# q, k, v loads on two DMA queues and matmuls on a zero tile between the first attention stages of a fused retention and MLP kernel

## The chip, the cores and the metric

One Trainium2 chip, one core of it. The metric is the time of one execution on the device in microseconds (us); lower is better. Most executions agree within 0.3%; each run is marked fast or slow, and only fast runs are compared. A profile is one more execution with the hardware profiler. Its "span" runs from the first to the last instruction and is about 2 us shorter than the time (252.3 against 254.3 here).

Names in the profile: PE is the matmul engine, PEld its weight loads, DVE, ACT and POOL the vector, scalar and general engines, SP the sync engine, which only issues DMA transfers. A DMA transfer issued by POOL goes to queue q0 ("software"), one issued by SP to q1 ("hardware"). L103 is line 103 of the kernel.

## The reference

```python
q, k, v: [4, 8, 768, 64] float32      # batch, heads, time, head size
gamma = 1 - 2 ** (-5 - arange(8))     # decay per head
for t in range(768):
    state = gamma * state + outer(k[t], v[t])
    y[t]  = q[t] @ state / sqrt(64)
x = y as [3072, 512]
h = x @ w_in                          # [512, 2048]
out = (h * cos(h)) @ w_out            # [2048, 512]
```

## The kernel before

The recurrence is computed in blocks of 128 time steps. A "pair" is one block of two batch items; there are 12 pairs. Each pair has six loads of 256 KB (q, k, v, two batch items each). Pairs 0 and 1 go through the attention first. Then six groups follow, of 16 steps each; a step computes one block of the first product (`unit_f`) and part of the second one for the group before (`unit_o`), and the attention of the next two pairs is woven in: `conv` (scaling of q and v on POOL), `stage_t` (transposes), `stage_a`/`stage_m` (masked scores), `stage_y`.

Every load is issued by POOL, and POOL does its work strictly in program order:

```python
    def load_pair(p):
        bp, c = divmod(p, NC)
        for t, src in ((qf, q), (kf, k), (vf, v)):
            for b in range(2):
                nc.gpsimd.dma_start(
                    out=t[p % PRE][:, b],
                    in_=src[2 * bp + b, :, ds(c * C, C)].rearrange("h t d -> t h d"))
# ... load_pair(0), constants (cut)
    load_pair(1)
    for r in range(2):
        load_w_in(r)
    conv_q(0, nc.vector)
    conv_k(0, True)
    conv_v(0, nc.gpsimd)
    stage_t(0)
    for r in range(2, 4):
        load_w_in(r)
    m0 = stage_a(0)
    conv_q(1, nc.vector)
    conv_k(1, True)
    conv_v(1, nc.gpsimd)
    for it in m0:
        stage_m(0, it)
    stage_t(1)
    stage_y(0)
    m1 = stage_a(1)
    for it in m1:
        stage_m(1, it)
    load_pair(2)
    load_pair(3)
    stage_y(1)
    for r in range(4):
        load_w_out(r)
    load_pair(4)

    def conv(p):
        conv_q(p, nc.gpsimd)
        conv_k(p, False)
        conv_v(p, nc.gpsimd)

    todo = []
    for g in range(NG + 1):
        for s in range(16):
            hf, r = divmod(s, 8)
            p = 2 * (g + 1) + hf
            if g < NG:
                unit_f(g, s)
            if g > 0:
                unit_o(g - 1, *divmod(s, 4))
            if p < NP:
                if r == 0:
                    conv(p)
                elif r == 1:
                    stage_t(p)
# ... stage_a, stage_m at r 2 and 3 (cut)
                elif r == 6:
                    stage_y(p)
                    if p + 3 < NP:
                        load_pair(p + 3)
```

A q, k or v load moves pieces of 64 float32, 256 bytes. A `w_in` or `w_out` load reads 1 MB and converts it to bfloat16, 512 KB written.

## Time and profile before

| | before |
|---|---|
| time, median | 254.37 us (254.3 to 255.47) |
| span of the profile | 252.3 us |
| PE idle before pair 2 | 22.2 us |
| POOL's multiply of q of pair 2 starts | 49.89 us |
| first transposes of pair 2 on PE | 51.00 us |
| first `unit_f` of the second group | 72.94 us |

Four rows of the page's slices of the kernel before: the span in 40 equal parts of 6.3 us, each digit the busy share in tenths, PEclk the granted clock of PE in tenths, GB/s what the DMA engines moved.

```profile
PE   0447400099798999999999999999999999999994
POOL 8999476498999999998330423000000000000000
PEclk9999755569999999999999999999999999999999
GB/s 110 218 212 207 233 218 209 206 235 219 221 158 222 158 194 223 188 168 221 108 0 44 42 44 1 42 47 42 3 42 44 42 0 44 42 42 42 44 83 83
```

PE is nearly full from the 13th slice on, and idle in slices 6 to 8; the DMA engines are full all through that gap, at 206 to 218 GB/s, and POOL is at work too. So the question is what holds up PE's start. The waits view of the kernel before (who waited for whom: us in total, how often, longest) has one long wait of PE:

```profile
PE bank_67 L162 <- POOL qs_98 L141: 22.2, 1, 22.2
```

qs_98 is q of pair 2, scaled on POOL. The timeline of POOL in the kernel before (start, length, what, and in brackets the idle time before it and what ended it) shows what POOL did instead:

```profile
30.92 0.88 POOL L103 DMA_DIRECT2D kf_89<-in_k_dram  x1 [0.32 <-DMA qf_83<-in_q_dram]
...
46.11 0.88 POOL L103 DMA_DIRECT2D vf_95<-in_v_dram  x1 [1.25 <-DMA w_out_sb<-in_moe_w_out_dram]
48.99 0.88 POOL L103 DMA_DIRECT2D vf_95<-in_v_dram  x1 [2.00 <-DMA w_out_sb<-in_moe_w_out_dram]
49.89 2.05 POOL L141 TENSOR_TENSOR qs_98<-qf_83,gq 128x512 bf16<-128x512 f32 x2
```

POOL issues loads and waits between them. The wait in front of kf_89 ended with the landing of qf_83, issued eight loads earlier; the same holds at every such wait, so at most eight of POOL's loads are under way. The last load ahead of the multiply, vf_95, is number 38 and could be issued when number 30, a w_out load, had landed. The data of pair 2 were there much earlier: the chain of waits has the landing of its last load (vf_93) at 36.7 us. The windows view of the kernel before (busy us of each engine in a stretch, granted clock, DMA share, GB/s) shows the engines' rate in that time:

```profile
core 0: us, PE busy (x) PEld busy (x) DVE busy (x) ACT busy (x) POOL busy (x), PEclk, DMA share, GB/s
30.00:40.00 10.00, 0.00 (x0) 0.00 (x0) 1.29 (x2) 0.00 (x0) 7.01 (x9) 0.56 1.05 219
40.00:50.00 10.00, 0.00 (x0) 0.00 (x0) 0.00 (x0) 0.00 (x0) 5.54 (x8) 0.50 1.19 205
```

And the DMA view for the first 49.9 us of the kernel before, that is up to the multiply:

```profile
DMA packets 5690, 10.06 MB, mean 202 GB/s; under 512 B 495, under 2 KB 4153, under 8 KB 5689
```

10.06 MB had been moved when PE could go on. The view counts bytes written, so a `w_in` or `w_out` load counts as 0.52 MB although it reads twice that; all MB and GB/s below are meant so.

### The profile page before, as it was taken

What the parts mean: (1) busy time and instruction counts of PE and PEld (TensorE: products, weight loads), DVE (VectorE), ACT (ScalarE), POOL (GpSimd) and SP (SyncE); (2) the same over time, 40 slices, a digit from 0 to 9 for tenths busy, and PEclk for the clock granted to TensorE, in tenths of its full rate; (3) what the DMA queues carried; (4) which work ended last, traced back from release to release, by engine and by line L of the source; (5) the groups of instructions that cost most, each with busy time, mean ns of one, the idle gap of its engine ahead of it and who ended that gap; (6) DMA issues with size and microseconds to landing.
All of it is one profiled execution on the core that took longest, in us unless ns stands there. A gap on an engine that the chain in (4) does not pass through costs nothing.

```text
span 252.3 us, 4113 instructions
## 1 busy us (share of the span) xinstructions
PE 204.9 (81%) x1640; PEld 107.4 (43%) x1664; DVE 119.1 (47%) x191; ACT 120.1 (48%) x174; POOL 116.8 (46%) x132
## 2 busy tenths in 40 slices
PE   0447400099798999999999999999999999999994
PEld 0336200055354455554455545545555454444441
DVE  4166320029685666347555665375556633343100
ACT  2434500047665556464565565645655554445210
POOL 8999476498999999998330423000000000000000
PEclk9999755569999999999999999999999999999999
DMA  4999999999979689779301110111011101111122
GB/s 110 218 212 207 233 218 209 206 235 219 221 158 222 158 194 223 188 168 221 108 0 44 42 44 1 42 47 42 3 42 44 42 0 44 42 42 42 44 83 83
DMA packets 13458, 29.62 MB, mean 117 GB/s; under 512 B 1664, under 2 KB 5760, under 8 KB 13440
## 3 DMA queue, kind: packets, MB, share of 16 engines
q0 software_dynamic: 9984, 23.07, 44.1%
q1 hardware_dynamic: 3456, 6.29, 6.7%
q8 instruction: 13, 0.21, 0.3%
q14 instruction: 5, 0.04, 0.1%
HBM read 27.26 MB, written 6.29 MB: 133 GB/s over the span
## 4 chain that ended last, share of the span: by engine, by line
PE 67%; POOL 15%; DMA 10%; issue 5%; DVE 1%; ACT 0%; POOLq 0%; ACTq 0%
PE bank_66 L246 14%; PE bank_63 L246 6%; PE bank_65 L232 5%; DMA vf_93<-in_v_dram 5%; PE bank_64 L232 5%; DMA w_out_sb<-in_moe_w_out_dram 5%; PE bank_69 L232 4%; PE bank_67 L232 4%; PE bank_68 L232 4%; PE bank_67 L246 4%; PE bank_63 L232 3%; PE bank_68 L246 3%; PE bank_69 L246 3%; POOL vs_103 L146 1%; POOL vs_102 L146 1%
## 5 line engine op out<-in xcount | busy, mean ns | idle before, releaser
L232 PEld LDWEIGHTS <-w_in_sb 128*128 128x128 bf16 x384 | 36.0, 99 | 40.8 <-issue 2.0
L246 PEld LDWEIGHTS <-gt_120 128*128 128x128 bf16 x192 | 18.8, 98 | 22.6
L246 PEld LDWEIGHTS <-gt_121 128*128 128x128 bf16 x192 | 18.8, 98 | 22.6
L246 PE MATMUL bank_66<-w_out_sb,gt_120 128*128 128x512 bf16 x96 | 24.6, 379 | 0.0
L162 PE MATMUL bank_67<-ident,qs_98 128*128 128x128 bf16 x8 | 1.0, 264 | 22.2 <-POOL qs_98 L141 22.2
L235 ACT ACTIVATE cosb_122<-bank_65,halfpi 128x512 bf16<-128x512 f32 x14 | 9.6, 687 | 14.5 <-PE bank_65 L232 14.5
L246 PE MATMUL bank_66<-w_out_sb,gt_121 128*128 128x512 bf16 x64 | 16.4, 379 | 0.0
L246 PE MATMUL bank_63<-w_out_sb,gt_120 128*128 128x512 bf16 x63 | 16.2, 379 | 0.1
L163 ACT COPY qkt_107<-bank_67 128x1024 bf16<-128x1024 bf16 x2 | 2.0, 1012 | 23.2 <-PE bank_67 L162 23.2
L162 PEld LDWEIGHTS <-qs_98 128*128 128x128 bf16 x32 | 2.4, 106 | 23.6 <-POOL qs_98 L141 22.9
L246 PE MATMUL bank_67<-w_out_sb,gt_121 128*128 128x512 bf16 x48 | 11.8, 379 | 0.0
L236 DVE TENSOR_TENSOR gt_120<-bank_69,cosb_124 128x512 bf16<-128x512 f32 x3 | 2.0, 683 | 19.9 <-ACT cosb_124 L235 19.9
L232 PE MATMUL bank_69<-xt_119,w_in_sb 128*128 128x512 bf16 x44 | 11.3, 379 | 0.0
L225 DVE CAST stb_117<-st_ps 64x512 bf16<-64x512 f32 x12 | 8.2, 687 | 5.7 <-PE st_ps L220 5.5
L235 ACT ACTIVATE cosb_124<-bank_64,halfpi 128x512 bf16<-128x512 f32 x9 | 6.2, 687 | 9.7 <-PE bank_64 L232 9.7
L232 PE MATMUL bank_63<-xt_118,w_in_sb 128*128 128x512 bf16 x40 | 10.3, 379 | 0.0
L232 PE MATMUL bank_65<-xt_119,w_in_sb 128*128 128x512 bf16 x34 | 8.8, 379 | 0.3 <-issue 0.3
L232 PE MATMUL bank_67<-xt_119,w_in_sb 128*128 128x512 bf16 x34 | 8.8, 379 | 0.3 <-issue 0.3
L232 PE MATMUL bank_64<-xt_119,w_in_sb 128*128 128x512 bf16 x34 | 8.8, 379 | 0.3 <-issue 0.3
L232 PE MATMUL bank_65<-xt_118,w_in_sb 128*128 128x512 bf16 x28 | 8.2, 405 | 0.9 <-issue 0.7
L246 PE MATMUL bank_68<-w_out_sb,gt_120 128*128 128x512 bf16 x32 | 8.2, 379 | 0.0
L246 PE MATMUL bank_69<-w_out_sb,gt_121 128*128 128x512 bf16 x32 | 8.2, 379 | 0.0
(324 smaller groups left out, 517.8 us busy)
## 6 DMA issues: line engine op xcount, KB each, us to landing
w_in_sb<-in_moe_w_in_dram POOLq DMA_DIRECT2D x4, 512.0 KB, 9.8
w_out_sb<-in_moe_w_out_dram POOLq DMA_DIRECT2D x4, 512.0 KB, 12.1
qf_81<-in_q_dram POOLq DMA_DIRECT2D x6, 256.0 KB, 4.3
kf_86<-in_k_dram POOLq DMA_DIRECT2D x6, 256.0 KB, 5.0
vf_91<-in_v_dram POOLq DMA_DIRECT2D x6, 256.0 KB, 5.5
qf_82<-in_q_dram POOLq DMA_DIRECT2D x6, 256.0 KB, 5.1
kf_87<-in_k_dram POOLq DMA_DIRECT2D x6, 256.0 KB, 5.8
vf_92<-in_v_dram POOLq DMA_DIRECT2D x6, 256.0 KB, 6.4
```

The costliest lines, as they stand in the source:

```text
L146: eng.tensor_tensor(out=vs[p % NB][:, b], in0=vf[p % PRE][:, b], in1=bc(gk, p % NC), op=ALU.mult)
L162: nc.tensor.transpose(tr[:, w, a, :], src[:, b, 2 * a : 2 * a + 2, :], ident)
L163: nc.scalar.copy(out=qkt[n][:, b], in_=tr)
L225: nc.vector.tensor_copy(out=stb[(p + 1) % 2][ts(j, 64), :, :, ts(j, 64)], in_=st_ps[ts(j, 64)])
L232: nc.tensor.matmul(bank, lhsT=w_in_sb[:, i, ts(f, 128)], rhs=xt[g % 2][:, i, :], start=(i == 0), stop=(i == KIN - 1))
L235: nc.scalar.activation(out=cb, in_=bank, func=AF.Sin, bias=halfpi)
L236: nc.vector.tensor_tensor(out=gt[g % 2][:, f, :], in0=bank, in1=cb, op=ALU.mult)
L246: nc.tensor.matmul(bank, lhsT=gt[g % 2][:, f, ts(j, 128)], rhs=w_out_sb[:, f, :], start=(f == 0), stop=(f == KOUT - 1))
```

## The change

The intent is twofold: to take half of the loads off POOL, so that issuing and waiting for them costs POOL less and two queues feed the DMA engines; and to keep PE's clock up through the short attention stages of pairs 0 and 1 with matmuls on a tile of zeros. With it come a new place for the w_in loads in the program and one copy moved from ACT to DVE. The diff:

```diff
--- before.py
+++ after.py
@@ -67,6 +67,15 @@
     st_ps = psum.tile([128, 2, HP, D], FP32, name="st_ps")
 
     ident = sb([128, 128], BF16, "ident")
+    zer = sb([128, 512], BF16, "zer")
+    nc.vector.memset(zer, 0.0)
+
+    def warm(n):
+        bank = banks.take()
+        for _ in range(n):
+            nc.tensor.matmul(bank, lhsT=zer[:, :128], rhs=zer, start=True, stop=True)
+        banks.give(bank)
+
     mask = sb([128, 128], BF16, "mask")
     pos = sb([128, NC], FP32, "pos")
     lgp = sb([128, NC, H], FP32, "lgp")
@@ -98,9 +107,11 @@
 
     def load_pair(p):
         bp, c = divmod(p, NC)
-        for t, src in ((qf, q), (kf, k), (vf, v)):
+        for t, src, engs in ((qf, q, (nc.sync, nc.sync)),
+                             (kf, k, (nc.gpsimd, nc.gpsimd)),
+                             (vf, v, (nc.sync, nc.gpsimd))):
             for b in range(2):
-                nc.gpsimd.dma_start(
+                engs[b].dma_start(
                     out=t[p % PRE][:, b],
                     in_=src[2 * bp + b, :, ds(c * C, C)].rearrange("h t d -> t h d"))
 
@@ -152,7 +163,7 @@
         else:
             nc.vector.tensor_copy(out=ks[p % NB], in_=kf[p % PRE])
 
-    def stage_t(p):
+    def stage_t(p, split):
         n = p % NB
         for b in range(2):
             bank = banks.take()
@@ -160,7 +171,10 @@
             for w, src in enumerate((qs[n], ks[n])):
                 for a in range(HP):
                     nc.tensor.transpose(tr[:, w, a, :], src[:, b, 2 * a : 2 * a + 2, :], ident)
-            nc.scalar.copy(out=qkt[n][:, b], in_=tr)
+            if split and b == 1:
+                nc.vector.tensor_copy(out=qkt[n][:, b], in_=tr)
+            else:
+                nc.scalar.copy(out=qkt[n][:, b], in_=tr)
             banks.give(bank)
 
     def qt(n, b, a):
@@ -254,28 +268,34 @@
 
 
     load_pair(1)
-    for r in range(2):
-        load_w_in(r)
+    load_w_in(0)
+    warm(14)
     conv_q(0, nc.vector)
     conv_k(0, True)
     conv_v(0, nc.gpsimd)
-    stage_t(0)
-    for r in range(2, 4):
-        load_w_in(r)
+    stage_t(0, True)
+    warm(3)
+    load_w_in(1)
+    load_w_in(2)
     m0 = stage_a(0)
+    warm(6)
+    for it in m0:
+        stage_m(0, it)
     conv_q(1, nc.vector)
     conv_k(1, True)
     conv_v(1, nc.gpsimd)
-    for it in m0:
-        stage_m(0, it)
-    stage_t(1)
+    load_w_in(3)
+    stage_t(1, True)
+    warm(3)
     stage_y(0)
     m1 = stage_a(1)
+    warm(8)
     for it in m1:
         stage_m(1, it)
     load_pair(2)
     load_pair(3)
     stage_y(1)
+    warm(4)
     for r in range(4):
         load_w_out(r)
     load_pair(4)
@@ -298,7 +318,7 @@
                 if r == 0:
                     conv(p)
                 elif r == 1:
-                    stage_t(p)
+                    stage_t(p, False)
                 elif r == 2:
                     todo = stage_a(p)
                     stage_m(p, todo[0])
```

## The prediction

> **What bounds the kernel.** From about 78 us to the end (252.3) the chain of waits is almost all PE: groups of four 128x512 matmuls at 0.86 us, no idle. Nothing in the change touches that part. What can move is when it starts. The timeline shows PE idle from 28.8 to 51.0 us; what ends the wait is qs_98 on POOL (the waits view: 22.2 us for this one wait). POOL could not start that multiply before 49.89 although q, k, v of pair 2 had all landed by about 37: in program order it stands behind the loads of pair 3, w_out and pair 4, and each POOL load waits for the one eight issues earlier (kf_89 waits for qf_83; the last vf_95 waits for the second w_out load). So POOL reaches the multiply when load 30 of 38 has landed. In that time the DMA engines are full: the windows view shows a DMA share of 1.05 to 1.21 and 205 to 221 GB/s from 12 to 60 us. A 256 KB q/k/v load costs 1.2 us of all 16 engines, a w load (512 KB written) 2.55 us. After that, 51 to 73 us, the first 16 output blocks take 21.9 us for about 18.1 us of PE work, because PE runs at half clock until 56.4 and because POOL needs 9.5 us per pair (4.1 multiply + 5.4 issue).
>
> **What the change does.** Per pair, three of six loads leave POOL for SP. Ahead of the multiply of pair 2 POOL now issues 23 loads, not 38, and with the same rule of eight waits for load 15 (a k of pair 3), with no w_out load ahead of it: 11 q/k/v loads (13 us) and 4 w_in (10.2 us) plus start, issue and landing. SP runs ahead with the q and half the v of pairs 0 to 6 (up to 21 loads) and competes. If a load costs the same on SP, and all 21 go first, the multiply starts near 54; if they share, near 40. The trace suggests sharing: POOL's 4 KB packets take 159 ns for some 50 to 80 packets after a pause and 302 to 314 ns in steady flow, so a single queue seems to leave half the engines' capacity unused. The Trainium skill ("DMA: Bandwidth & Descriptors", "Issuing engines are not separate DMA queues") says more issuing engines save only sequencer time; I expect total GB/s above 221 in this head nevertheless. POOL per pair falls to about 6.8 us, so it stops delaying PE afterwards.
>
> **Warm matmuls.** 38 of 128x512, at most 0.43 us each, stand in a head that ends around 25 to 30 us, before PE waits anyway. The last four end more than 8 us before pair 2 arrives, so PE is cold again by then ("TensorE: Matmul & The Clock Gate", "The HAM clock gate": half clock after an idle window of about 3.4 us; here 0.5 was granted after the stall began, till 56.4). I expect 0 us from them, within 1. The copy moved from ACT to DVE: also 0.
>
> **Sum.** Multiply of pair 2: 49.9 -> about 40.5 (9.4 us gained, range 0 to 16). First 16 blocks: 21.9 -> about 19.5 (2.4 gained). Rest unchanged at 179.4 + 2 outside the span. 254.3 - 11.8 = **242.5 us**, range 234 to 252. Chances: faster by over 2% 0.82, within 0.14, slower 0.04.
>
> **Signs.** Right: qs of pair 2 starts at 36 to 45 us, PE idle before it is under 17 us, head traffic over 240 GB/s, PE still shows 0.86 us groups at the end. Wrong: the SP loads' 256-byte pieces take the engines from POOL's queue (w_in late, k of pair 3 landing after 50), or SP is slow (over 3 us per load) and POOL waits for q of pair 2 or 4.

## The result, and the profile after

| | before | after |
|---|---|---|
| time, median | 254.37 us | 246.57 us (246.19 to 247.1) |
| span of the profile | 252.3 us | 244.9 us |
| PE idle before pair 2 | 22.2 us | 13.0 us |
| multiply of q of pair 2 starts | 49.89 us | 42.84 us |
| first transposes of pair 2 (A) | 51.00 us | 43.95 us |
| first `unit_f` of the second group (B) | 72.94 us | 65.77 us |
| from A to B | 21.94 us | 21.82 us |
| from B to the end of the span | 179.4 us | 179.1 us |

The ratio is 0.9685 (95% interval 0.9653 to 0.9717). A ratio is the mean time of one kernel's fast runs over that of the other's of the same rounds, so it is not quite the ratio of the medians. The changed kernel is 3.1% faster. The table says where: of 7.4 us of span, 7.05 are gained before PE starts pair 2, 0.1 between A and B, 0.2 after.

The same slices of the changed kernel (6.1 us each):

```profile
PE   7358900897999999999999999999999999999993
POOL 8620885985089994373306015000000000000000
PEclk9875985599999999999999999999999999999999
GB/s 157 220 203 197 193 227 208 195 211 225 216 200 246 231 170 158 185 108 195 43 102 88 29 161 57 1 44 45 43 3 43 43 45 11 32 43 45 73 56 86
```

PE now restarts in the eighth slice. The row of GB/s is not higher than before; POOL's row has a hole in slices 3 and 4. The waits view and POOL's timeline of the changed kernel:

```profile
PE bank_65 L173 <- POOL qs_100 L152: 13.0, 1, 13.0
```

```profile
12.45 1.56 POOL L119 DMA_DIRECT2D w_in_sb<-in_moe_w_in_dram  x2
25.38 2.04 POOL L157 TENSOR_TENSOR vs_105<-vf_94,gk 128x512 bf16<-128x512 f32 x2 [11.37 <-DMA vf_94<-in_v_dram]
27.37 0.81 POOL L119 DMA_DIRECT2D w_in_sb<-in_moe_w_in_dram  x1
...
41.95 0.88 POOL L114 DMA_DIRECT2D vf_97<-in_v_dram  x1 [0.32 <-DMA kf_91<-in_k_dram]
42.84 2.05 POOL L152 TENSOR_TENSOR qs_100<-qf_85,gq 128x512 bf16<-128x512 f32 x2
```

The multiply (now qs_100) stands behind 23 loads, and the last one, vf_97, waited for kf_91, a k of pair 3 and number 15 of POOL's loads; no w_out load had to land first. The new hole is the line at 25.38: POOL stood for 11.37 us until v of pair 1 came, whose first half is now loaded by SP. The windows and the DMA view of the changed kernel for the time up to its multiply:

```profile
30.00:40.00 10.00, 1.00 (x5) 0.27 (x3) 1.98 (x3) 1.37 (x2) 6.93 (x9) 0.73 1.13 220
40.00:50.00 10.00, 6.04 (x43) 3.53 (x44) 1.55 (x3) 3.12 (x4) 8.34 (x10) 0.58 1.19 196
50.00:60.00 10.00, 8.60 (x106) 4.83 (x104) 7.81 (x13) 7.58 (x12) 8.66 (x9) 1.00 1.15 220
```

```profile
DMA packets 15554, 8.59 MB, mean 201 GB/s; under 512 B 12499, under 2 KB 14785, under 8 KB 15553
q0 software_dynamic: 3310, 5.49, 67.1%
q1 hardware_dynamic: 12243, 3.09, 43.3%
```

The mean rate up to the multiply is 201 GB/s, against 202 before. What differs is the amount: 8.59 MB instead of 10.06. Divided by the rate, 1.47 MB is 7.3 us; the multiply came 7.05 us earlier. At an equal rate this division must come out nearly so, whatever the cause; what it shows is that the rate did not rise. The fairer comparison is at the same moment, the DMA view of the kernel before for its first 42.8 us:

```profile
DMA packets 4211, 8.59 MB, mean 201 GB/s; under 512 B 447, under 2 KB 2674, under 8 KB 4210
```

By then both kernels have moved 8.59 MB. The changed one moves more in the first 12 us (187 against 161 GB/s) and less from 12 to 42.8 us. So the two queues brought no more bytes; the loads that POOL's multiply stands behind were only fewer, and done sooner.

Two more readings. First, the packets. The third part of the page, before and then after (packets, MB, share of 16 engines' time):

```profile
q0 software_dynamic: 9984, 23.07, 44.1%
q1 hardware_dynamic: 3456, 6.29, 6.7%
```

```profile
q1 hardware_dynamic: 40896, 15.73, 29.3%
q0 software_dynamic: 7104, 13.63, 27.7%
```

36 loads moved from q0 to q1. q0 lost 2,880 packets, 80 a load, and q1 gained 37,440, 1,040 a load. A load has 1,024 pieces of 256 bytes: on SP's queue each is a packet of its own, with 16 more to close the load; 80 fits 64 packets of 4 KB, sixteen pieces each, and the same 16. Second, how the queues share. The DMA view of the changed kernel from 17.5 to 25 us, when POOL has w_in loads (packets of 1 KB) under way and SP its q and v:

```profile
q0 software_dynamic: 1143, 1.12, 88.1%
q1 hardware_dynamic: 1346, 0.34, 32.1%
```

About one packet of one queue for each of the other, so SP gets a quarter of the bytes. The Trainium skill ("DMA: Bandwidth & Descriptors", "Queues, rings and completion order") says that an engine takes turns between its queues packet by packet; this trace agrees, with 1,346 packets to 1,143.

The stretch from A to B, in the windows view of before and of after:

```profile
51.00:72.94 21.94, 19.88 (x212) 11.37 (x217) 14.94 (x25) 14.69 (x21) 21.27 (x23) 0.91 1.05 224
```

```profile
43.95:65.77 21.82, 20.42 (x216) 11.47 (x217) 14.82 (x25) 14.69 (x21) 13.68 (x14) 0.90 1.15 213
```

POOL was busy for 21.3 of 21.9 us before and for 13.7 of 21.8 after, and the stretch is as long as it was.

### The profile page after: what moved, and what is told of

Read it like the earlier page. It is cut to its first block, busy times and chain, and to the rows that moved or that the text cites. A ratio compares the mean times of both kernels' runs of the same rounds, so it can differ in the third digit from the quotient of the medians.

```text
span 244.9 us, 4252 instructions
## 1 busy us (share of the span) xinstructions
PE 216.7 (88%) x1702; PEld 109.6 (45%) x1702; DVE 120.0 (49%) x194; ACT 118.3 (48%) x172; POOL 85.0 (35%) x96
## 4 chain that ended last, share of the span: by engine, by line
PE 72%; DMA 12%; DVE 6%; POOL 3%; issue 2%; SPq 2%; ACT 1%; DVEq 0%; ACTq 0%; POOLq 0%
PE bank_63 L260 14%; DMA vf_94<-in_v_dram 8%; PE bank_68 L260 6%; PE bank_69 L246 5%; PE bank_67 L246 5%; PE bank_64 L246 5%; PE bank_66 L246 5%; PE bank_65 L246 5%; PE bank_65 L260 4%; DMA kf_91<-in_k_dram 4%; PE bank_68 L246 4%; PE bank_67 L260 3%; PE bank_66 L260 3%; DVE gt_122 L250 2%; SPq L114 2%
## 5 line engine op out<-in xcount | busy, mean ns | idle before, releaser
L260 PE MATMUL bank_63<-w_out_sb,gt_122 128*128 128x512 bf16 x96 | 24.6, 379 | 0.0
L260 PE MATMUL bank_63<-w_out_sb,gt_123 128*128 128x512 bf16 x64 | 16.4, 379 | 0.0
L260 PE MATMUL bank_68<-w_out_sb,gt_122 128*128 128x512 bf16 x64 | 16.4, 379 | 0.0
L260 PE MATMUL bank_65<-w_out_sb,gt_123 128*128 128x512 bf16 x48 | 11.8, 379 | 0.0
L246 PE MATMUL bank_67<-xt_121,w_in_sb 128*128 128x512 bf16 x44 | 11.3, 379 | 0.0
L246 PE MATMUL bank_68<-xt_120,w_in_sb 128*128 128x512 bf16 x40 | 10.3, 379 | 0.0
L246 PE MATMUL bank_64<-xt_121,w_in_sb 128*128 128x512 bf16 x36 | 9.3, 380 | 0.0
L246 PE MATMUL bank_69<-xt_121,w_in_sb 128*128 128x512 bf16 x36 | 9.3, 380 | 0.0
L246 PE MATMUL bank_65<-xt_121,w_in_sb 128*128 128x512 bf16 x36 | 9.3, 380 | 0.0
L173 PEld LDWEIGHTS <-qs_100 128*128 128x128 bf16 x32 | 2.4, 106 | 14.4 <-POOL qs_100 L152 13.7
L246 PE MATMUL bank_69<-xt_120,w_in_sb 128*128 128x512 bf16 x32 | 8.2, 380 | 0.0
L246 PE MATMUL bank_64<-xt_120,w_in_sb 128*128 128x512 bf16 x32 | 8.2, 380 | 0.0
L246 PE MATMUL bank_66<-xt_120,w_in_sb 128*128 128x512 bf16 x32 | 8.2, 380 | 0.0
L260 PE MATMUL bank_66<-w_out_sb,gt_122 128*128 128x512 bf16 x32 | 8.2, 379 | 0.0
```

Of the source, the lines that this page charges most:

```text
L173: nc.tensor.transpose(tr[:, w, a, :], src[:, b, 2 * a : 2 * a + 2, :], ident)
L246: nc.tensor.matmul(bank, lhsT=w_in_sb[:, i, ts(f, 128)], rhs=xt[g % 2][:, i, :], start=(i == 0), stop=(i == KIN - 1))
L260: nc.tensor.matmul(bank, lhsT=gt[g % 2][:, f, ts(j, 128)], rhs=w_out_sb[:, f, :], start=(f == 0), stop=(f == KOUT - 1))
```

## The experiments

The theory after the result: (A) PE starts earlier because fewer bytes are queued ahead of POOL's multiply of pair 2; the DMA engines move some 200 GB/s whoever issues. Rivals: (W) the matmuls on zeros bring part of it; (C) the second queue moves more bytes per us. All kernels gave correct results. Runs e1 to e4, then e5 to e8 and then the rest shared a chip and the runs of the kernel before. The changed kernel itself was timed in another call, so it is compared with them through their ratios to the kernel before.

### e1: without the zero matmuls

```diff
-    warm(14)      # and the five other calls, and the tile zer
```

> The changed kernel without the 38 matmuls on the zero tile. Theory A (the gain is that POOL has 23 instead of 38 loads ahead of the multiply of pair 2, and the warm matmuls lie in a head where PE waits anyway): multiply of pair 2 on POOL still at 42 to 44 us, time within 1 us of the changed kernel's 246.6. Rival W (the warm matmuls bring part of the gain): over 2 us slower, 249 or more.

Measured: 246.7 us, ratio 0.9689 (0.964 to 0.9737), against 0.9685 with them. The multiply came at 41.09 us, a little earlier than the range given; the profiled run was the fastest of four (244.98). The profile that was kept, of another execution (span 245.5 us), has the multiply at 43.18, inside the range: this moment varies by 2 us between executions of one kernel, so differences under 2 us between single profiles say little. W is out: the 38 matmuls are worth nothing that the interval, about 0.5% to either side, could show.

### e2: zero matmuls and new program order, all loads on POOL

```diff
-        for t, src, engs in ((qf, q, (nc.sync, nc.sync)), ...
+        for t, src in ((qf, q), (kf, k), (vf, v)):      # all on nc.gpsimd, as before
```

> The kernel before, with the warm matmuls, the moved copy and the new order of the w_in loads, but all q, k, v loads on POOL. Theory A: 38 loads stand ahead of the multiply of pair 2 again, it starts at 49 to 51 us, time 253.5 to 255.5, as before. Rival W: 251 or less.

Measured: 255.48 us, ratio 1.0028 (0.999 to 1.0067), both as theory A expected. POOL's timeline in e2 at the multiply:

```profile
49.77 2.05 POOL L150 TENSOR_TENSOR qs<-qf,gq 128x512 bf16<-128x512 f32 x2
```

The rest of the change does nothing; all of the gain comes from moving loads off POOL. This does not yet say whether it is the order or the second queue.

### e3 and e3b: POOL does not stand before v of pair 1

```diff
-    conv_v(1, nc.gpsimd)
...
     load_pair(2)
     load_pair(3)
+    conv_v(1, nc.gpsimd)
     stage_y(1)
```

> The changed kernel with POOL's multiply of v of pair 1 put behind the loads of pairs 2 and 3, so that POOL does not stand for 11.4 us (14.0 to 25.4 us) with w_in and pair 2 unissued. Theory A1 (this stand is why the multiply of pair 2 came at 42.8 and not 40.5): it starts at 38 to 40, and the time falls by 2 to 4 us. Rival B (the DMA engines are full at some 205 GB/s whoever issues, so what POOL's queue gets earlier the SP queue gets later): q of pair 4, which landed at 68.4 us just as PE needed it at 69.2, comes no earlier; PE then stalls at pair 4, and the time falls by less than 1.5 us.

Measured: 248.37 us, unclear (246.38 to 250.66), and the profiled run was a slow one. So it was run again:

> The same kernel as e3 again, since its profiled run was a slow one and its times scattered from 246.4 to 250.7. If the scatter belongs to the kernel (two queues in a race for the same engines): again 246 to 251, not faster than the changed kernel's 246.6. If it was chance: within 1 us of one value. What POOL gains by not standing before v of pair 1 is expected to be lost waiting for q of pair 2 or 4 from SP.

Measured again: 247.65 us (247.07 to 248.75), ratio 0.9733 (0.9691 to 0.9774); the profile is of a fast run. POOL's timeline in it:

```profile
24.93 2.04 POOL L157 TENSOR_TENSOR vs<-vf,gk 128x512 bf16<-128x512 f32 x2 [1.51 <-DMA vf<-in_v_dram]
...
37.44 1.05 POOL L152 TENSOR_TENSOR qs<-qf,gq 128x512 bf16<-128x512 f32 x1
42.47 1.04 POOL L152 TENSOR_TENSOR qs<-qf,gq 128x512 bf16<-128x512 f32 x1 [3.98 <-DMA qf<-in_q_dram]
49.05 2.04 POOL L157 TENSOR_TENSOR vs<-vf,gk 128x512 bf16<-128x512 f32 x2 [5.54 <-DMA vf<-in_v_dram]
```

A1 was right about the first half: it is multiplied at 37.44, even before its range of 38 to 40. But the second half then waits 3.98 us for q from SP, and the v multiply 5.54 us more. Nothing is gained; the interval overlaps the changed kernel's (0.9653 to 0.9717) and lies rather above it. B's claim that what POOL's queue gains SP's loses holds; its place was wrong, as the loss shows at pair 2 already and not at pair 4.

### e4: one queue, another order

```diff
     load_pair(1)
-    for r in range(2):
-        load_w_in(r)
+    load_w_in(0)
...
     stage_t(0)
-    for r in range(2, 4):
-        load_w_in(r)
...
     load_pair(2)
+    load_w_in(1)
     load_pair(3)
     stage_y(1)
-    for r in range(4):
-        load_w_out(r)
-    load_pair(4)
...
                 if r == 0:
                     conv(p)
+                    if p == 2:
+                        load_w_in(2)
+                        load_w_in(3)
+                    elif p == 3:
+                        for i in range(4):
+                            load_w_out(i)
+                        load_pair(4)
...
-                    if p + 3 < NP:
-                        load_pair(p + 3)
+                    if p == 3:
+                        load_pair(5)
+                    elif 3 < p and p + 2 < NP:
+                        load_pair(p + 2)
```

> The kernel before with one queue and no warm matmuls, only the order of POOL's work changed: pair 2 is loaded right after one w_in piece, its multiply stands behind 26 loads and ahead of the last two w_in pieces, w_out and pair 4. Theory A (order on POOL is what counts, not the number of queues): multiply of pair 2 at 27 to 31 us; then pair 4, behind all of w_in and w_out, lands at about 60 to 63 us and its transposes, at 78.5 us before and 69.2 in the changed kernel, come at 62 to 65. Time 238 to 244, faster than the changed kernel with no second queue. Rival C (the second queue itself moves more bytes per us): no faster than 250.

Measured: 242.66 us (242.49 to 243.78), ratio 0.9551 (0.9514 to 0.9587). With one queue and no zero matmuls it is faster than the changed kernel. POOL's timeline and the DMA view up to the multiply in e4:

```profile
26.01 1.79 POOL L103 DMA_DIRECT2D qf<-in_q_dram  x2
27.77 1.78 POOL L103 DMA_DIRECT2D kf<-in_k_dram  x2
29.52 1.91 POOL L103 DMA_DIRECT2D vf<-in_v_dram  x2
31.44 2.06 POOL L141 TENSOR_TENSOR qs<-qf,gq 128x512 bf16<-128x512 f32 x2
...
51.26 0.88 POOL L103 DMA_DIRECT2D vf<-in_v_dram  x1 [2.37 <-DMA w_out_sb<-in_moe_w_out_dram]
...
61.95 2.05 POOL L141 TENSOR_TENSOR qs<-qf,gq 128x512 bf16<-128x512 f32 x2
```

```profile
DMA packets 2477, 5.80 MB, mean 185 GB/s; under 512 B 313, under 2 KB 1314, under 8 KB 2476
```

5.80 MB instead of 10.06 have been moved when the multiply starts at 31.44, just past the expected range of 27 to 31. The rate is no higher (185, as the slow start of the first 12 us weighs more). But the multiply does not wait for bytes here: from 19.94 to 31.44 POOL issues 13 loads one after the other, some 0.9 us each, with no wait for a landing, and multiplies at once. In e4 it is the issuing of the loads ahead that sets the start; before and after the change it is their landing, for every wait shown there ends with one. So the count of loads ahead is no measure by itself: the changed kernel has 23 ahead against 26 here and starts 11 us later, as its POOL stood 11.37 us for v of pair 1 and then waited for landings among w_out and pair 4. The multiply of pair 4 comes at 61.95 and its transposes at 63.06, as expected: the wait has partly moved to there. C is out as the main cause.

### e5: zero matmuls in the gap itself

```diff
                 elif r == 1:
+                    if p == 2:
+                        warm(50)
                     stage_t(p, False)
```

> The changed kernel with 50 more matmuls on the zero tile, placed in the gap in which PE waits for pair 2 (31 to 44 us), ahead of its transposes. Theory H (after the start the first 16 output blocks still take 21.8 us because PE runs at half clock for its first 5.9 us, not because of POOL): the clock stays at 1.0 through the start, the 16 blocks take 18.5 to 20, time 243.5 to 245.5, that is 1 to 3 us less than the changed kernel. Rival P (the 16 blocks are paced by POOL or the hand-overs between engines): still 21 to 22 us, time within 0.7 us of 246.6.

Measured: 246.56 us (245.89 to 249.5), ratio 0.9705 (0.9639 to 0.9771): no gain, so P held and not H; the stretch from A to B took about 21.5 us in its trace. The windows view of e5 for the gap and for just after the start:

```profile
31.00:44.90 13.90, 11.40 (x58) 5.44 (x58) 1.36 (x3) 0.32 (x2) 9.93 (x13) 0.95 1.15 216
45.00:48.30 3.30, 3.30 (x29) 1.75 (x29) 0.32 (x1) 2.48 (x3) 3.30 (x4) 0.72 1.22 196
```

The clock was not at 1.0 through the start: PE still waited 2.4 us between the last zero matmul and the transposes, and half clock was granted from about 43.4 to 46.9 us (mean 0.72 from 45 to 48.3). So e5 is only half a test; e6 is the better one.

### e8 and e8b: no w_in packets while SP loads pair 1

```diff
-    load_w_in(1)
-    load_w_in(2)
     m0 = stage_a(0)
...
     conv_v(1, nc.gpsimd)
+    load_w_in(1)
+    load_w_in(2)
     load_w_in(3)
```

> The changed kernel with the second and third w_in load put behind POOL's multiply of v of pair 1, so that no w_in packets run while SP brings q and v of pair 1. Theory S (the engines serve the two queues one packet in turn, and an SP packet is 256 bytes against 1024 of w_in and 4096 of q/k/v on POOL, so SP's loads crawl whenever POOL's queue is full): v of pair 1 is there by 14 to 19 us, not 25.4. Rival O (SP's loads are slow by themselves): still 23 to 26. The whole time, since the bytes stay the same, within 3 us of 246.6 by both.

Measured: 248.45 us (247.52 to 254.59), the profiled run slow. Again:

> The same kernel as e8 again, for a fast profile (times 247.5 to 254.6 before). Theory S: v of pair 1 used by POOL at 14 to 21 us, earlier than the 25.4 of the changed kernel, and the multiply of pair 2 later than 42.8, since w_in then comes later: time 247 to 250. Rival O: v of pair 1 at 23 to 26.

Measured again: 247.51 us (246.65 to 249.62), ratio 0.9734 (0.9678 to 0.9791). The profile is of a fast run; POOL's timeline in it:

```profile
19.63 2.04 POOL L157 TENSOR_TENSOR vs<-vf,gk 128x512 bf16<-128x512 f32 x2 [7.31 <-DMA vf<-in_v_dram]
...
42.39 2.05 POOL L152 TENSOR_TENSOR qs<-qf,gq 128x512 bf16<-128x512 f32 x2
```

v of pair 1 is there at 19.63 instead of 25.38 (just past the 19 of e8, within the 21 of e8b), so S holds: SP's loads were slow because of POOL's packets. The multiply of pair 2 came at 42.39, not later than 42.84 as expected; and the time is no better. The stand at 25.38 looked like a cost of 11 us; shortening it to 1.51 us (e3b) or to 7.31 us (e8b) brought nothing.

### e6: e4 with zero matmuls in its two gaps

```diff
                 elif r == 1:
+                    if p == 2:
+                        warm(14)
+                    elif p == 4:
+                        warm(18)
                     stage_t(p)
```

> The kernel with one queue and the changed order (242.7), plus 14 matmuls on the zero tile ahead of the transposes of pair 2 and 18 ahead of those of pair 4, where that kernel's PE stands for 3.6 and 4.3 us and then runs at half clock. Theory H: 1 to 3 us less, 239.5 to 241.5. Rival P: within 0.7 us of 242.7.

Measured: 241.64 us (241.04 to 242.38), ratio 0.9491 (0.9454 to 0.9528), 1.0 us below e4 by the medians, just outside the range given; the two intervals overlap a little. The stretch from A to B in e4, then in e6:

```profile
32.56:55.15 22.59, 21.19 (x216) 11.65 (x217) 14.86 (x25) 14.69 (x21) 18.09 (x20) 0.87 1.17 206
```

```profile
32.68:54.08 21.40, 18.21 (x214) 10.23 (x218) 15.28 (x25) 14.61 (x21) 16.93 (x20) 1.00 1.16 198
```

With the clock at 1.0 throughout the stretch takes 21.4 us, 1.2 less than in e4 at a mean of 0.87. PE is busy for 18.2 of them; the rest are short waits for other engines and for one w_in piece. So the half clock costs about 1 us here, not 2 to 3.

### e7 and e9: e4, the attention of pair 4 later, and SP for pair 0 alone

```diff
-                nc.gpsimd.dma_start(
+                eng = nc.sync if p == 0 and (t is qf or (t is vf and b == 0)) else nc.gpsimd
+                eng.dma_start(
...
-                elif r == 1:
+                elif r == (3 if p == 4 else 1):
                     stage_t(p)      # and stage_a, stage_m, stage_y of pair 4: r 4, 4 and 5, 7
```

> The kernel with one queue and the changed order (242.7), plus two things: q and half of v of pair 0 alone on SP, where nothing else is in flight, and the attention of pair 4 two output blocks later, since its load lands last. Expected: loads 1 to 2 us earlier, and the stand of PE before pair 4 (4.3 us, then 3.4 us at half clock) shrinks to under 1.5 us: time 237.5 to 240.5. If the loads' end were not what PE waits for there, no change from 242.7.

Measured: 237.2 us (236.72 to 239.96), ratio 0.9351 (0.9285 to 0.9418), a little better than expected. PE's wait before pair 4 fell from 4.3 to 2.25 us, less than hoped. e9 takes SP away again:

> The fastest kernel (237.2) with all loads on POOL again, so the new order and the later attention of pair 4 alone. If SP is worth only the earlier start of the first loads (1.3 us, multiply of pair 2 at 29.95 against 31.44): 238 to 239.5. If the second queue is worth more: 240 or more.

Measured: 239.12 us (238.03 to 239.33), ratio 0.9378 (0.9336 to 0.9421), as expected if SP only lets the first loads start earlier. So the new order and the later pair 4 bring 6.2% of time without a second queue. SP for the first three loads adds 1.9 us between medians; the intervals overlap, so its size is not settled.

### e10: e7 with zero matmuls in its gaps

```diff
+                    if p == 2:
+                        warm(14)
+                    elif p == 4:
+                        warm(8)
                     stage_t(p)
```

> The fastest kernel (237.2) plus 14 matmuls on the zero tile in the gap before pair 2 and 8 before pair 4. In e6 matmuls so placed kept the clock at 1.0 and brought 1.0 us between the medians; here half clock is granted from 32.1 to 35.5, just after the start: 235.5 to 237, 0.5 to 1.5 us less.

Measured: 237.31 us (236.62 to 237.7), ratio 0.9318 (0.9283 to 0.9353). This is outside the 235.5 to 237 that was expected, and there is no difference from e7 beyond the intervals. e7 and e10 beat both the kernel before and the changed kernel, by 17 and 9 us.

## Why the prediction was right or wrong

The time, 246.57 us, lies in the range of 234 to 252, and "faster" was right. The gain was 7.8 us instead of 11.8. The range was wide, 0 to 16 us for the start of the multiply alone, so that the time lies in it owes something to luck: both terms of the sum were too large, and POOL's stand of 11.37 us before v of pair 1 was not foreseen.

- **What bounds the start: right.** "in program order it stands behind the loads of pair 3, w_out and pair 4". e2 and e4 show it from both sides: with 38 loads ahead, the multiply comes at 49.77 us; with 26 and the same single queue, at 31.44 (there after their issuing, not their landing).
- **That POOL would wait for load 15, a k of pair 3: right.** The timeline shows vf_97 waiting for kf_91.
- **"a single queue seems to leave half the engines' capacity unused", total above 221 GB/s, sign at 240: wrong.** Up to the multiply the mean was 201 GB/s with two queues, 202 with one. (The 221 was no ceiling either: the kernel before moves 229 GB/s from 50 to 60 us, a stretch that the prediction counts within its 205 to 221.) I had set this expectation against the sentence of the Trainium skill ("DMA: Bandwidth & Descriptors", "Issuing engines are not separate DMA queues") that more issuing engines only save sequencer time; the runs agree with the page. The fast packets after a pause are real, but did not turn into rate. The term of the start was mis-sized accordingly: 9.4 us expected, 7.05 measured (from single profiles, which in e1 differ by 2 us). The 8.59 MB that went ahead would have needed 38.9 us at 221 GB/s (an estimate); they took 42.8.
- **"First 16 blocks: 21.9 -> about 19.5": wrong.** It measured 21.8, so this term was 2.3 us too large. I had put the loss down to POOL's 9.5 us per pair and to half clock. POOL became free for 8 of 22 us and nothing changed, so POOL was not the pace there; half clock stayed (mean 0.58 from 40 to 50 us, 1.00 from 50 on) because the new warm matmuls end before the wait, and even a full clock (e6) leaves 21.4 us.
- **Warm matmuls worth 0: right** (e1, e2). The Trainium skill ("TensorE: Matmul & The Clock Gate", "The HAM clock gate") has the clock fall back after an idle window of about 3.4 us; the trace agrees nearly: PE computes two more blocks after the last of them, stops at about 30.9 us for 13 us, and half clock is granted from 34.8, 3.9 us later, to 48.4.
- **Rest unchanged: right**, 179.4 and 179.1 us.
- **What would make it wrong: partly seen.** "the SP loads' 256-byte pieces take the engines from POOL's queue" is the wrong way round. POOL's larger packets kept SP's loads waiting (e8b).

What stays open: why the engines carry about 200 GB/s of these pieces on either queue, and why the stretch from A to B keeps 3 us of small waits at full clock; they were not taken apart. How much of the 7.05 us comes from bytes no longer ahead, and how much from the 15 issues of some 0.9 us that POOL is spared, was not separated; e4 shows that issuing alone can set the start. That e3b and e8b are no faster than the changed kernel fits the full DMA engines, but only the waits named were shown.

## What to carry to other kernels

When the DMA engines are full during the start, count what stands ahead of the first thing that the bounding engine needs, the bytes as well as the time to issue the loads, and reorder the loads so that there is less; a second queue helped here mainly as far as it changed this order, and it can starve if its packets are smaller. On an engine that both issues loads and computes, a limit on the loads under way makes program order a lock: keep the multiply that others wait for ahead of loads that are not yet needed. Matmuls that keep the clock up belong directly before the work that ends the wait, and a look at what the half clock costs there comes first: they brought 1.0 us by the medians in e6 and nothing in e10.

## What the Trainium skill lacked or had wrong

- "DMA: Bandwidth & Descriptors": it says engines take turns by packet, but not that on SP's queue every 256-byte piece is a packet of its own (1,040 packets for a 256 KB load, against 80 on POOL's queue), so that SP got 0.34 MB while POOL's w_in loads got 1.12 MB.
- The same page has no rate on trn2 for loads in pieces of 256 bytes mixed with weight loads that are converted; these runs show about 200 GB/s of bytes written with one queue or two (202 and 201).
- No page that was read says that at most eight of POOL's loads are under way; the trace shows it (kf_89 waits for qf_83, vf_95 for a w_out load). Whether it is the chip's or the framework's limit was not tested.
- "TensorE: Matmul & The Clock Gate": it names an idle window of about 3.4 us; in e5 less was enough: half clock was granted again from about 43.4 us, 2.2 us after the last matmul on zeros ended and before the transposes that ended the gap (43.72). In e7 a gap of 2.25 us before pair 4 left the clock at 1.0, so the length of the gap alone does not decide it; these are single traces. Matmuls on zeros do hold the clock: 1.0 over the whole stretch in e6.
